# Padding the row counts of DMA loads to multiples of 16 or 15, and issuing a second table behind the first on one queue

## Chip, cores, metric

One core of one Trainium2 chip. The metric is the device time of one execution in microseconds (us), lower is better.

## The reference, cut to what matters

```python
X = np.fft.fft(np.fft.fft(x, axis=1), axis=2).real   # x: (8, 3008, 256) float32
h = X.reshape(24064, 256) @ w_in                     # (256, 2048)
g = np.maximum(h, 0.0) ** 2
out = g @ w_out                                      # (2048, 256)
```

The kernel folds the symmetric parts of the sequence together, multiplies by cosine and sine tables on TensorE, and then runs the two-layer block. Eight batches follow one another; while one is in the block, the next one's transform is slipped in between.

## The kernel before: what the change and the argument touch

```python
def class_tiles(S):                 # S = 3008: rows of x in 7 tiles by residue class
    half = S // 8 + 1
    tiles = []
    for c, order in enumerate((range(0, half, 4), range(2, half, 4), range(1, half, 2), range(half, S // 4 + 1))):
        for r in range(0, len(order), P):
            tiles.append((c, order[r], order.step, len(order[r:r + P])))
    return tiles                    # row counts: 95, 94, 128, 60, 128, 128, 120
...
    def load_x(b, t):
        _, r0, step, rows = TILES[t]

        pool, tag = (gp, "g") if b == 0 and t < NT - NX else (xp, "x")
        xt[b, t] = pool.tile([P, 4, D], F32, name="xt", tag=tag)
        nc.sync.dma_start(out=xt[b, t][0:rows], in_=x[b, r0:r0 + step * (rows - 1) + 1:step])
...
    for t in range(NT):
        load_x(0, t)

    def load_table(tab, src, engine):

        for t, (c, r0, step, rows) in enumerate(TILES):
            for i, (s0, count) in enumerate(row_tiles(S)):
                mine = [...]        # rows of this source tile that belong to tile t
                if mine:
                    o = (s0 + mine[0] - r0) // step
                    nk = NC[0][c]
                    engine.dma_start(out=tab[o:o + len(mine), :, PLACE[t]:PLACE[t] + nk],
                                     in_=src[mine[0]:mine[-1] + 1:step, :, i, 0:nk])

    load_table(cosT, cos_s, nc.sync)
    make_identity(nc, ident)
    load_table(sinT, sin_s, nc.gpsimd)
...
    for t in range(4):
        for_p(t)                    # VectorE folds four x tiles
    groups_at(0, 4)                 # TensorE: cosine products of the first classes
    for_p(4)
    groups_at(1, 2)                 # VectorE joins them (ScalarE has copied one part)
    for_p(5)
    ...
```

A row of an x tile is one run of 4096 bytes. A table is loaded in twelve pieces, of 32, 32, 31, 32, 32, 30, 64, 64, 60, 128, 128 and 120 rows; the first nine serve the first product. After the tables the sync queue loads the weights.

## Time and profile before

| | before |
|---|---|
| median time, 4 runs | 2087.41 us (2086.92 to 2092.67) |
| span of the profiled run | 2090.3 us |
| granted TensorE clock, mean | 0.987 |
| first matmul | 33.14 us |
| ScalarE's first copy of a product | 36.02 us |

In these lines PE is TensorE, DVE VectorE, ACT ScalarE, POOL GpSimd, and SPq the sync engine's queue of DMA issues. A profile line of a wait reads: who waited, for whom, us in total, times, longest. The page's account of the DMA queues has packets, MB and the share of 16 engines; q1 is the hardware queue that sync feeds, q0 the software queue of GpSimd:

```profile
q1 hardware_dynamic: 64030, 65.06, 10.7%
q0 software_dynamic: 752, 1.57, 0.3%
```

q0 holds the sine table and nothing else. Two instructions serve as milestones below: ScalarE's first copy (the first product is done) and the start of VectorE's second conversion of a raw weight (its second instruction that writes fd from raw: the head's folds and joins are done, the phase that converts weights has begun). Timeline lines have start, length, engine, line, operation and tiles:

```profile
36.02 0.24 ACT L353 COPY da<-pd 128x95 f32<-128x95 f32 x1 [34.00 <-PE pd L345]
```
```profile
64.01 0.42 DVE L201 TENSOR_SCALAR fd<-raw 128x512 uint32<-128x512 uint32 x1
```

### The profile page before, as it was taken

The numbers are of one execution on the slowest core, as the hardware profiler recorded it, in microseconds if no ns is written. First come the engines' busy times: TensorE is split into PE (matmuls) and PEld (weight loads), VectorE is DVE, ScalarE is ACT, GpSimd is POOL, SyncE is SP. The second block draws the span as 40 slices with busy tenths as digits, with TensorE's granted clock in tenths as the row PEclk, the third lists the DMA queues.
The fourth block names the chain that finished last, engine by engine and source line by source line (L and its number), as shares of the span: only waits on it lengthen the run. The fifth ranks groups of instructions, "written<-read, shape, count | busy, mean of one in ns | idle before, by whom it ended". The sixth has DMA issues, their size and how long they took to land.

```text
span 2090.3 us, 27087 instructions
## 1 busy us (share of the span) xinstructions
PE 2011.9 (96%) x9464; PEld 1748.1 (84%) x9464; DVE 1333.7 (64%) x3271; ACT 949.2 (45%) x1069; POOL 1211.9 (58%) x1778
## 2 busy tenths in 40 slices
PE   3789999999999999999999999999999999999997
PEld 1578887888888888888888888888888888888887
DVE  4688855777557765677556775577656775555553
ACT  0364434454445444444444544454444454344443
POOL 1157644676457665566546765576646665456654
PEclk9789999999999999999999999999999999999999
DMA  6124100010001000110000110011001100000000
GB/s 164 61 77 56 46 10 26 25 45 31 10 31 40 29 27 11 40 40 26 30 26 25 37 38 11 25 41 32 28 11 38 42 11 19 27 11 10 21 11 20
DMA packets 64918, 68.35 MB, mean 33 GB/s; under 512 B 25802, under 2 KB 55519, under 8 KB 64782
## 3 DMA queue, kind: packets, MB, share of 16 engines
q1 hardware_dynamic: 64030, 65.06, 10.7%
q0 software_dynamic: 752, 1.57, 0.3%
q8 instruction: 74, 1.21, 0.2%
q14 instruction: 62, 0.51, 0.1%
HBM read 41.93 MB, written 24.68 MB: 32 GB/s over the span
## 4 chain that ended last, share of the span: by engine, by line
PE 94%; DVE 3%; DMA 2%; ACT 1%; issue 0%; POOL 0%; POOLq 0%; ACTq 0%; SPq 0%; DVEq 0%
PE ph L405 16%; PE ph L406 16%; PE mA L445 16%; PE mC L445 15%; PE mB L445 15%; PE mD L445 8%; PE pd L345 5%; PE po L479 2%; DMA xt<-in_x_dram 1%; PE pg L229 1%; ACT os L481 0%; DMA cosT<-in_cos_s_dram 0%; PE pe L235 0%; DVE fd L211 0%; DVE fs L213 0%
## 5 line engine op out<-in xcount | busy, mean ns | idle before, releaser
L419 ACT ACTIVATE g<-g 128x1004 f32<-128x1004 f32 (+1 forms) x384 | 399.4, 1040 | 832.3 <-DVE g L411 549.9
L408 DVE SCALAR_TENSOR_TENSOR he<-Et,gE,ph 128x251 f32<-128x251 f32 (+1 forms) x768 | 361.9, 471 | 596.7 <-PE ph L406 596.1
L425 POOL TENSOR_TENSOR s<-g 128x251 f32<-128x251 f32 (+1 forms) x384 | 251.6, 655 | 688.7 <-ACT g L420 661.9
L405 PE MATMUL ph<-Pt,G 128*128 128x251 f32 (+1 forms) x1536 | 455.4, 377 | 0.4 <-DVE g L411 0.4
L406 PE MATMUL ph<-Qt,G 127*128 127x251 f32 (+1 forms) x1536 | 453.7, 376 | 0.0
L420 ACT ACTIVATE g<-g 128x1004 f32<-128x1004 f32 (+1 forms) x384 | 399.3, 1040 | 12.1
L445 PE MATMUL mA<-g,wout 128*128 128x251 f32 (+1 forms) x1536 | 389.9, 375 | 0.0
L445 PE MATMUL mC<-s,wsum 128*128 128x251 f32 (+1 forms) x1536 | 389.4, 374 | 0.0
L410 DVE TENSOR_TENSOR g<-he,ph 128x251 f32<-128x251 f32 (+1 forms) x768 | 320.5, 417 | 58.9 <-DVE he L408 0.5
L405 PEld LDWEIGHTS ph<-Pt,G 128*128 128x128 f32 x1536 | 289.4, 190 | 42.5 <-issue 3.2
L406 PEld LDWEIGHTS ph<-Qt,G 127*128 127x128 f32 x1536 | 292.9, 191 | 36.6
L445 PEld LDWEIGHTS mC<-s,wsum 128*128 128x128 f32 x1536 | 291.6, 190 | 35.2
L445 PEld LDWEIGHTS mA<-g,wout 128*128 128x128 f32 x1536 | 285.5, 189 | 40.1 <-issue 4.0
L411 DVE TENSOR_TENSOR g<-he,ph 128x251 f32<-128x251 f32 (+1 forms) x768 | 314.1, 409 | 0.0
L426 POOL TENSOR_TENSOR s<-s,g 128x251 f32<-128x251 f32 (+1 forms) x384 | 288.0, 750 | 30.1
L427 POOL TENSOR_TENSOR s<-g 128x251 f32<-128x251 f32 (+1 forms) x384 | 291.2, 758 | 0.0
L428 POOL TENSOR_TENSOR s<-g,s 128x251 f32<-128x251 f32 (+1 forms) x384 | 262.9, 685 | 0.0
L445 PE MATMUL mB<-g,wsum 128*128 128x251 f32 (+1 forms) x768 | 225.1, 374 | 0.0
L445 PE MATMUL mD<-s,wout 128*128 128x251 f32 (+1 forms) x768 | 225.0, 374 | 0.0
L445 PE MATMUL mB<-s,wout 128*128 128x251 f32 (+1 forms) x768 | 224.6, 374 | 0.0
L445 PEld LDWEIGHTS mB<-g,wsum 128*128 128x128 f32 x768 | 145.6, 190 | 17.8
L445 PEld LDWEIGHTS mD<-s,wout 128*128 128x128 f32 x768 | 144.9, 189 | 18.1
(74 smaller groups left out, 1327.8 us busy)
## 6 DMA issues: line engine op xcount, KB each, us to landing
xt<-in_x_dram SPq DMA_DIRECT2D x24, 512.0 KB
out_dram<-os SPq DMA_DIRECT2D x96, 125.0 KB
out_dram<-os SPq DMA_DIRECT2D x80, 126.0 KB
Et<-e_dram SPq DMA_DIRECT2D x7, 752.5 KB
raw<-in_moe_w_in_dram SPq DMA_DIRECT2D x16, 256.0 KB
raw<-in_moe_w_out_dram SPq DMA_DIRECT2D x16, 256.0 KB
xt<-in_x_dram SPq DMA_DIRECT2D x8, 480.0 KB
xt<-in_x_dram SPq DMA_DIRECT2D x8, 380.0 KB
```

Source lines behind the costliest of these rows:

```text
L405: nc.tensor.matmul(hP, G1[:, fs], pt[:, ks], start=True, stop=True)
L406: nc.tensor.matmul(hQ, G2[:, fs], qt[:, ks], start=True, stop=True)
L408: nc.vector.scalar_tensor_tensor(out=t, in0=et[:, ks], scalar=gE[:, fc:fc + 1], in1=hP, op0=ALU.mult, op1=ALU.add)
L410: tt(out=g[:, h, 0, 0:n], in0=t, in1=hQ, op=ALU.add)
L411: tt(out=g[:, h, 1, 0:n][:, ::-1], in0=t, in1=hQ, op=ALU.subtract)
L419: act(v, v, AF.Relu)
L420: act(v, v, AF.Square)
L425: gt(out=s1, in0=g21, in1=g22, op=ALU.add)
L426: gt(out=s2, in0=s1, in1=g11, op=ALU.subtract)
L427: gt(out=s3, in0=g11, in1=g21, op=ALU.subtract)
L428: gt(out=s4, in0=g12, in1=s2, op=ALU.subtract)
L445: nc.tensor.matmul(acc[nm][:, i, 0:n], w, v[:, 0:n], start=j == 0 and i == 0, stop=j == NJ - 1, skip_group_check=True)
```

## The change

Intent: let each load of x and each table piece run on all the DMA engines, by loading one or two rows more that nothing reads, and keep the sine table, which is needed late, from competing with x and the cosine table.

```diff
     def load_x(b, t):
         _, r0, step, rows = TILES[t]
 
+        while rows % 15 and rows % 16 and r0 + step * rows < NROW:
+            rows += 1
+
@@ load_table
-                    o = (s0 + mine[0] - r0) // step
+                    o, m = (s0 + mine[0] - r0) // step, len(mine)
+                    while m % 15 and m % 16 and o + m < P and mine[0] + step * m < P:
+                        m += 1
                     nk = NC[0][c]
-                    engine.dma_start(out=tab[o:o + len(mine), :, PLACE[t]:PLACE[t] + nk],
-                                     in_=src[mine[0]:mine[-1] + 1:step, :, i, 0:nk])
+                    engine.dma_start(out=tab[o:o + m, :, PLACE[t]:PLACE[t] + nk],
+                                     in_=src[mine[0]:mine[0] + step * (m - 1) + 1:step, :, i, 0:nk])
@@
-    load_table(sinT, sin_s, nc.gpsimd)
+    load_table(sinT, sin_s, nc.sync)
```

The loads of 95 and 94 rows become 96 in every batch, and the table piece of 31 rows becomes 32. Nothing else changes its shape.

## The prediction

> **What bounds the kernel now.** I began with the page's chain (part 4) to see which engine sets the end, then read the waits and the table of stretches to see where TensorE does not run, then the chain in order of time for that place alone, then the waits of the DMA queue to see why.
>
> ```profile
> PE 94%; DVE 3%; DMA 2%; ACT 1%; issue 0%; POOL 0%; POOLq 0%; ACTq 0%; SPq 0%; DVEq 0%
> ```
>
> TensorE is the bound of the whole, and DMA holds 2% of the chain. The stretches of time (us, then busy us per engine, granted clock, DMA share, GB/s) say where that 2% lies:
>
> ```profile
> 0.00:10.00 10.00, 0.00 (x0) 0.00 (x0) 1.86 (x7) 1.28 (x1) 7.21 (x16) 1.00 0.68 171
> 10.00:20.00 10.00, 0.00 (x0) 0.00 (x0) 0.00 (x0) 0.00 (x0) 1.80 (x3) 1.00 1.04 214
> 25.00:33.00 8.00, 0.00 (x0) 0.00 (x0) 6.70 (x20) 0.00 (x0) 0.00 (x0) 1.00 0.21 62
> 60.00:90.00 30.00, 22.61 (x71) 16.05 (x71) 14.15 (x32) 10.38 (x23) 0.00 (x0) 0.68 0.16 53
> 1000.00:1100.00 100.00, 98.65 (x464) 84.19 (x463) 53.04 (x141) 42.50 (x48) 51.27 (x79) 1.00 0.06 21
> ```
>
> No matmul runs before 33 us. Late in the kernel TensorE is 98.65 of 100 us busy and the DMA engines are at 0.06. So only the head can be shortened by faster transfers. Its waits, in total, times and longest (first two lines: compute engines; last: the sync DMA queue):
>
> ```profile
> PE pd L345 <- DMA cosT<-in_cos_s_dram: 33.1, 1, 33.1
> DVE fs L293 <- DMA xt<-in_x_dram: 22.2, 3, 16.4
> ```
> ```profile
> SPq L160 <- DMA xt<-in_x_dram: 16.9, 4, 13.6
> ```
>
> The third line is the key: the issue of the cosine table (L160) itself waits for a load of x. The chain in order of time (start, us):
>
> ```profile
> 1.18 23.59 DMA xt<-in_x_dram
> 24.77 0.02 issue
> 24.79 8.10 DMA cosT<-in_cos_s_dram
> ...
> 33.14 2.86 PE pd L345 x8
> ```
>
> One x load, issued at 1.18 us, lands at 24.77, and only then is a piece of the cosine table issued, which lands at 32.89. The trace names both: the load is the second, of 94 rows; the piece is the third of twelve, of 31 rows. The queue reuses eight completion semaphores in turn, so transfer number n waits for number n-8: piece 3 (transfer 10) waits for load 2.
>
> **What the Trainium skill says.** "DMA: Bandwidth & Descriptors", section "Why a DMA increments its semaphore by 16 and not by 1": the number of engines is the largest k up to 16 that divides the slowest dimension of both sides, on this path the lowest-numbered k; the queue writes the other 16-k counts at once. The trace agrees. The 95-row load shows one early update at 1.25 us and five from 5.73 to 6.53 (k=5); the 94-row load one at 1.59 and two, at 24.11 and 24.77 (k=2); the 31-row piece has k=1; 60 and 120 rows give 15. The same page, "Queues, rings and completion order", has an engine consume descriptors in ring order. That also shows: of the third load's 16 counts, 14 came between 6.40 and 9.06 and two at 26.46 and 26.86, behind the 94-row load on its two engines. The last x load had 13 engine counts by 20.32 and its last two at 30.87 and 31.34. Same page, "Issuing engines are not separate DMA queues": transfers from sync and GpSimd share the 16 engines; here the sine table's packets lie in the same microseconds (2 to 26) as those of x. "TensorE: Matmul & The Clock Gate", Part 1: the clock is halved until activity releases it; the trace has 0.68 granted in 60 to 90 us and 1.00 later.
>
> **The change part by part.**
> *Rows of x.* 95 and 94 become 96: six rows (4096 bytes each) on each of 16 engines instead of 19 on five and 47 on two. Engine 1 now carries 19+47+8+4+8+8+8 = 102 of the first batch's rows, an engine from 5 up 36. After, an engine carries 6+6+8+4+8+8+8 = 48. I counted packets in the trace in slices of 2 us: from 4 to 8 us, all engines at work, 4096-byte packets took 210 to 241 ns each and 504 and 451 KB of x moved per slice. So 48 rows take 48 x 0.24 = 11.5 us; packets flow from about 2.3 us, so the last x load lands at about 14.5 instead of 31.34. The extra row costs 12 KB in all, 0.05 us.
> *Rows of the table.* Only one piece changes, 31 rows to 32 (k 1 to 16); 30 rows stay at 15, the rest at 16 or 15. Its own 8.10 us (62 descriptors of 380 bytes behind engine 0's backlog) go below those of its neighbours.
> *Sine to the sync queue.* Twelve issues of about 0.63 us, 7.5 us of queue, and 1.52 MB move from beside x to after the cosine; at some 250 KB per us this is 6 us of transfer. It frees x of 1.57 MB of competing packets; GpSimd does not need its 12 issues' time.
>
> *What first sets TensorE going.* The first group needs nine cosine pieces. Pieces 8 and 9 are issued when the last x load and piece 1 have landed. Before: x complete 31.34, piece 9 issued 32.02, landed 34.26 (2.9 us after x), the first result copied by ScalarE at 36.02 (1.76 us more). After: 14.5 + 2.9 + 1.76 = 19.2. The gain at this point is 36.02 - 19.2 = 16.8 us; I take 16.
>
> *Does it last?* From 36 to 58 us the chain is VectorE folding and joining (14.05 of 15 us busy in 45 to 60), in fixed order, and it moves as a block. Next needs, each moved 16 us earlier: odd cosine product at 41.78, so 25.8; last cosine piece landed 39.91, 8.6 us after x, so 23.1: 2.7 us to spare. Sine product at 55.83, so 39.8; the last sine issues come at about 26 and land near 31: 8 us to spare. First weights used at 58.79, so 42.8; their issue moves from 36.6 to about 29 and they landed 5.4 us after issue, so 34.5: 8 us to spare. The next weights wait for x buffers that VectorE frees, so they move along. Nothing gives the 16 back, and after 137 us TensorE runs at full clock to the end. In later batches the x loads get shorter too, but TensorE waits for no DMA there: 0.
>
> Sum: 2087.3 - 16 = **2071 us**, 0.8% faster.
>
> **Rivals.**
> (1) *Sine in the way.* If its 7.5 us of issue stood before something needed, the gain would be 16 - 7.5 = 8.5: 2079 us. For it: the queue is one, in order, and weights stand behind. Against: the 8 us to spare above.
> (2) *Bandwidth.* If 16 engines at work slow each other: 10 to 20 us had 214 GB/s at share 1.04. Then 3.02 MB take 14.1 us, x lands at 16.4, the gain is 14: 2073. For it: 4096-byte packets took 240 to 290 ns with all engines at work and only some 150 with two. I put half of this in, by taking 16 and not 16.8.
> (3) *VectorE takes the place of DMA.* Its four folds before the first join last 7.1 us (26.88 to 28.68 is one, 1.8) and need loads 1 to 4. Load 4 ends with row 24 of 48, at 2.3 + 24 x 0.24 = 8, so folds end near 10, a fifth near 13, before 19.2. It would bind only if x came still faster; then no more than some 6 us would be left to win.
> (4) *Clock.* Between 52 and 137 us the clock alternates between half and full in steps of 3.4 us, 48 us at half in all. One such step more or less costs 3.4/2 = 1.7 us where TensorE is on the path. A moved phase can give 2 or 3 us either way; the runs before already spread from 2086.92 to 2092.67.
>
> **Range and chances.** 2071 with 2 us either way for the landing of x and 3 to 4 for clock and noise, more room upward for rival 1: 2065 to 2078. Two per cent is 41.7 us, more than the 33 us for which TensorE stands idle at the start, so faster by over 2% gets 0.01. Slower by 2% would need a new wait in the TensorE-bound part, to which the change adds nothing: 0.01. Same: 0.98.
>
> **What would show it.** Right: the seven loads of x land in order, the last near 14.5 us; the wait of the queue's L160 for x falls from one of 13.6 us to several of 1 or 2; the first matmul comes near 16 to 17 us and ScalarE's first copy near 19; the software queue q0 disappears; the sequence up to 137 us is the old one, 16 us earlier; the stretch 1000:1100 is unchanged. Wrong: a first matmul still waiting after 22 us (bandwidth or issue), a wait of TensorE or VectorE for the sine table or raw weights of some us (rival 1), or a head that is 16 us shorter while the total is not (clock or a wait later on).

## The result, and the profile after

The median of four runs is **2069.3 us** (2067.63 to 2071.05), against 2087.41 before. The ratio is 0.9908, 95% interval 0.989 to 0.9926. Ratios here are the mean time of one kernel's fast runs over that of the other's in the same rounds, so not quite the ratio of the medians quoted. By a 2% rule this is "the same"; the 0.9% is clear of the noise.

The page of the changed kernel has no q0 any more; the chain holds less DMA:

```profile
q1 hardware_dynamic: 65968, 66.73, 11.4%
```
```profile
PE 94%; DVE 3%; DMA 1%; ACT 0%; issue 0%; SPq 0%; POOL 0%; POOLq 0%; ACTq 0%; DVEq 0%
```

The waits up to 110 us, of the compute engines and then of the sync queue:

```profile
PE pd L350 <- DMA cosT<-in_cos_s_dram: 16.2, 2, 15.5
...
DVE fs L298 <- DMA xt<-in_x_dram: 4.0, 1, 4.0
```
```profile
SPq L165 <- DMA xt<-in_x_dram: 7.4, 7, 1.7
SPq L165 <- DMA cosT<-in_cos_s_dram: 1.1, 1, 1.1
```

TensorE's wait for the cosine table is halved, and the queue's four waits for x, one of them of 13.6 us, have become seven with a longest of 1.7. The chain in order of time:

```profile
3.51 11.18 DMA xt<-in_x_dram
14.71 2.52 DMA cosT<-in_cos_s_dram
17.23 0.14 issue
17.36 1.91 PE pd L350 x4
19.30 0.25 ACT da L358
```

The x load on the chain is now the last one, issued at 3.51, no longer the second. The cosine piece behind it is the eighth, which waits for the last load's completion count as before.

When each load of x was complete, from the semaphore updates in the two traces (us). A load is complete at 16 counts; each engine that carries part of it adds one when its part is there, and the counts that no engine will add come at once (the prediction shows this for loads of 95 and 94 rows). So the number of late counts is the number of engines:

| load | rows | engines before | complete before | rows after | complete after |
|---|---|---|---|---|---|
| 1 | 95 | 5 | 6.53 | 96 | 4.84 |
| 2 | 94 | 2 | 24.77 | 96 | 6.13 |
| 3 | 128 | 16 | 26.86 | 128 | 8.06 |
| 4 | 60 | 15 | 27.48 | 60 | 9.30 |
| 5 | 128 | 16 | 28.75 | 128 | 10.34 |
| 6 | 128 | 16 | 30.02 | 128 | 12.35 |
| 7 | 120 | 15 | 31.34 | 120 | 14.69 |

Five loads that the change does not touch end 17 to 19 us earlier. The milestone of the weights:

```profile
47.98 0.42 DVE L206 TENSOR_SCALAR fd<-raw 128x512 uint32<-128x512 uint32 x1
```

It is 16.03 us earlier than before. But the profiled spans differ by 23.2 us (2090.3 to 2067.1). Between about 64 and 140 us of the kernel before, the two profiles part by another 6.9 us. The stretches show where (columns as in the prediction's table of stretches: length, then busy us of PE, of PE's weight loads, of DVE, ACT and POOL; the clock is the third number from the end):

```profile
60.00:90.00 30.00, 19.24 (x68) 15.82 (x69) 23.42 (x44) 18.24 (x31) 9.10 (x15) 0.74 0.32 95
90.00:120.00 30.00, 25.47 (x117) 21.52 (x116) 27.63 (x49) 19.97 (x33) 15.67 (x24) 0.92 0.32 99
...
120.00:140.00 20.00, 20.00 (x99) 17.90 (x98) 18.25 (x38) 11.25 (x17) 15.16 (x25) 1.00 0.31 67
```

and the kernel before in the later two:

```profile
90.00:120.00 30.00, 21.37 (x68) 17.11 (x67) 24.15 (x44) 17.45 (x28) 12.81 (x21) 0.72 0.27 88
120.00:140.00 20.00, 17.94 (x75) 15.43 (x76) 17.45 (x31) 11.97 (x21) 10.50 (x16) 0.83 0.35 106
```

This profile of the kernel before had 47.8 us at half clock ahead of its steady part, that of the changed kernel 30.7. (The traces hold no record of the clock before 41.76 and 26.65 us; the 1.00 of earlier stretches is no measurement.) Four of the 6.9 us can be followed on the two chains: from the second weight conversion to the third they have the same links, and the same 14 matmuls took, before and after,

```profile
72.02 6.67 PE pd L345 x14
```
```profile
55.08 3.49 PE pd L350 x14
```

The clock records have half clock from 65.65 to 79.31 us in the first trace and full clock from 53.96 to 60.79 in the second. With two shorter groups of matmuls this makes 4.1 us, and the third conversion starts 20.1 us earlier instead of 16.0. The experiments show that which execution meets how much of this is chance and no part of the change. From 204 us on nothing more is won or lost: between fixed VectorE instructions the two traces differ by 22.92 us at 204 us, 22.87 at 537 and 22.86 at 1636, and the stretch from 1000 to 1100 us has the same busy TensorE:

```profile
1000.00:1100.00 100.00, 98.65 (x466) 85.09 (x466) 55.24 (x142) 42.86 (x49) 54.68 (x83) 1.00 0.07 21
```

### The profile page after: what moved, and what is told of

Same layout as the page of the kernel before. It is cut to its first block, busy times and chain, and to the rows that moved or that the text cites. A ratio compares the mean times of both kernels' runs of the same rounds, so it can differ in the third digit from the quotient of the medians.

```text
span 2067.1 us, 27083 instructions
## 1 busy us (share of the span) xinstructions
PE 2004.5 (97%) x9464; PEld 1742.9 (84%) x9464; DVE 1334.7 (65%) x3271; ACT 949.4 (46%) x1069; POOL 1202.6 (58%) x1766
## 4 chain that ended last, share of the span: by engine, by line
PE 94%; DVE 3%; DMA 1%; ACT 0%; issue 0%; SPq 0%; POOL 0%; POOLq 0%; ACTq 0%; DVEq 0%
PE ph L410 16%; PE mA L450 16%; PE ph L411 16%; PE mC L450 16%; PE mB L450 15%; PE mD L450 8%; PE pd L350 5%; PE po L484 2%; PE pg L234 1%; DMA xt<-in_x_dram 1%; ACT os L486 0%; DVE he L413 0%; PE pe L240 0%; DVE g L416 0%; DVE g L415 0%
## 5 line engine op out<-in xcount | busy, mean ns | idle before, releaser
L450 PEld LDWEIGHTS mD<-s,wout 128*128 128x128 f32 x768 | 144.9, 189 | 18.1
```

Of the source, the lines that this page charges most:

```text
L450: nc.tensor.matmul(acc[nm][:, i, 0:n], w, v[:, 0:n], start=j == 0 and i == 0, stop=j == NJ - 1, skip_group_check=True)
```

## The experiments

The theory: loads of 95 and 94 rows run on five and two engines; engines work in order, so every later transfer with a share on engines 0 and 1 waits behind them. Rivals: the sine packets beside x are the whole cause; the single-engine table piece is; the queue's wait for a completion count is; or a load lands by its bytes, whatever the engines. All heads are read from one profile a run; the spread of ScalarE's first copy is some 0.9 us (19.30 and 20.20 for the changed kernel, profiled twice). Times are medians. All outputs are right. The kernel before had 2086.68 us beside e1 to e4, 2087.43 beside e5 to e8, and 2087.02 beside e9 and e10 (the last is the seven runs of the second and one more).

### e1: x rows alone

```diff
 # from the changed kernel
-                    while m % 15 and m % 16 and o + m < P and mine[0] + step * m < P:
-                        m += 1
-    load_table(sinT, sin_s, nc.sync)
+    load_table(sinT, sin_s, nc.gpsimd)
```

> Only the rows of x are padded; table rows and the sine table (GpSimd queue) as before. Theory (the backlog of engines 0 and 1, made by the loads of 95 and 94 rows, holds the head): the last x load lands near 17.5 us instead of 31.3 (48 rows per engine, beside some 0.7 MB of sine), the 31-row piece of the cosine table on one engine costs some 2.5 us more, ScalarE's first copy comes at about 23.5 instead of 36.0: 12.5 us less, about 2075 us. Rival (the sine table's packets beside x are the main cause): x lands after 25 us, the first copy comes after 30, gain under 6 us.

Measured: 2078.53 us, ratio 0.9959 (0.9945 to 0.9974). The last x load was complete at 18.36; the first copy, in the timeline:

```profile
27.25 0.24 ACT L356 COPY da<-pd 128x95 f32<-128x95 f32 x1 [25.23 <-PE pd L348]
```

That is 8.8 us earlier than before, more than the sine rival allows and less than the 12.5 that I expected. x itself landed close to the 17.5 expected; the nine cosine pieces took 7.0 us more (25.35), against 3.0 in the whole change. They now move beside the large sine pieces, the last of which landed at 23.38, and the 31-row piece on one engine landed at 24.15; e5 tells the two apart in part.

### e2: table rows alone

```diff
 # from the kernel before
+                    while m % 15 and m % 16 and o + m < P and mine[0] + step * m < P:
+                        m += 1
```

> Only the one table piece of 31 rows is made 32, on both tables. Theory: nothing, as its 8.1 us on the chain were spent behind the backlog of engine 0 and its neighbours end no earlier: the first copy at 36.0 us as before (within 1), time within 2 us of the kernel before. Rival (the single-engine piece itself is slow): the first copy comes 3 us or more earlier.

Measured: 2084.66 us, ratio 0.9994 (0.9975 to 1.0013). The first copy came at 34.63, 1.4 us earlier, just outside what I expected and not far from the spread. But x, which this edit does not touch, was complete at 29.99 instead of 31.34, and the ninth cosine piece came 2.9 us after x, as before. So the whole 1.4 us came with x, and none of it behind x, where the cosine piece stands. Load 2 was in (24.14 instead of 24.77) before that piece was issued; the padded sine piece beside x, or chance, is what is left, and no run tells these apart.

### e3: sine table alone

```diff
 # from the kernel before
-    load_table(sinT, sin_s, nc.gpsimd)
+    load_table(sinT, sin_s, nc.sync)
```

> Only the sine table moves behind the cosine on the sync queue; x loads stay at 95 and 94 rows, the table piece at 31. Theory: engine 1 still carries 102 rows of x, at 0.2 us each while all engines work and 0.15 when two are left, so the last x load lands near 20 to 21 us, the first copy at about 25.5: some 10.5 us less, about 2077 us. If sine packets beside x cost nothing: the first copy stays at 36. Together with the x-only run this tells how far the two parts overlap: 12.5 and 10.5 do not add up to the 16.7 of both.

Measured: 2078.96 us, ratio 0.9968 (0.9949 to 0.9988). x complete at 23.02, first copy at 27.76: 8.3 us earlier. The chain of this run still has the 94-row load in it, shorter:

```profile
1.17 16.11 DMA xt<-in_x_dram
17.30 7.29 DMA cosT<-in_cos_s_dram
```

```profile
27.76 0.24 ACT L353 COPY da<-pd 128x95 f32<-128x95 f32 x1 [25.74 <-PE pd L345]
```

So the sine packets beside x did cost, and the rows too. The packets of the kernel before show how: from 22 to 26 us, 27 packets of x of 4096 bytes started, beside 18 large ones of the sine table; from 26 to 30 us, after the last sine packet (25.92), 49 did. Each took about as long in both stretches (170 and 163 ns on average); they took turns. I had expected the two parts to overlap; with 8.8 and 8.3 they add up to 17.1, and both together gave 16.7.

### e4: the change without its table rows

```diff
 # from the changed kernel
-                    while m % 15 and m % 16 and o + m < P and mine[0] + step * m < P:
-                        m += 1
```

> The change without its table rows: x padded, sine behind cosine, but the piece of 31 rows on one engine. Theory: 62 descriptors of 380 bytes on engine 0, about 40 ns each, put 2.5 us of backlog on that engine ahead of six cosine pieces: the first copy at about 21.3 us instead of 19.3, total about 2 us above the whole change (2071). Rival (31 rows or 32 are the same once x is even): the first copy within 0.5 us of 19.3.

Measured: 2072.34 us (2068.31 to 2076.73), ratio 0.9929 (0.9906 to 0.9952). My expectation was wrong: the first copy came at 19.28, not 21.3. The piece of 31 rows landed at 15.04, between its neighbours (14.94 and 15.22). The median above 2069 is the clock, told below: two of the four runs had it at 0.986.

### e5: the change with the sine table back on GpSimd

```diff
 # from the changed kernel
-    load_table(sinT, sin_s, nc.sync)
+    load_table(sinT, sin_s, nc.gpsimd)
```

> The change without its third part: x and table rows padded, the sine table still on the GpSimd queue beside x. In the x-only run (first copy 27.25 us) the 31-row piece of the cosine table landed at 24.15, 3.6 us after the piece before it, and the pieces behind it ended on that one engine at 24.3 to 25.35, while three engines lagged anyhow (24.17 for the next slowest). Theory: taking that piece off the one engine lets the ninth cosine piece land at about 24.2 and the first copy come at about 26.1, 1.1 us earlier than with x alone; the other 7 us to the whole change (19.3) come from the sine packets that still run until some 23 us. Rival (the one-engine piece is what held the x-only run): the first copy near 22.

Measured: 2078.84 us (2074.61 to 2082.94), ratio 0.9958 (0.9937 to 0.998). Two of its four runs were long ones (clock 0.986 and 0.987, told under e9), so the median says little beside that of e1. The first copy came at 26.35, where 26.1 was expected:

```profile
26.35 0.24 ACT L358 COPY da<-pd 128x95 f32<-128x95 f32 x1 [24.33 <-PE pd L350]
```

The rival is out: with all rows even, the sine table beside x and the cosine still costs 6.2 to 7.1 us (26.35 against 20.20 and 19.30). The number was reached by another way than I had thought, though: x was complete only at 20.49 (18.36 in e1, with the same x rows), and the ninth cosine piece, at 24.40, came 3.9 us after x instead of 7.0. So the even piece may well have saved some 3 us behind x, of which the later x took 2; one profile each does not settle it.

### e6: cosine table ahead of x

```diff
 # from the kernel before
-    for t in range(NT):
-        load_x(0, t)
     ...
     load_table(cosT, cos_s, nc.sync)
+    for t in range(NT):
+        load_x(0, t)
```

> From the kernel before, only the order: the cosine table is issued ahead of the x loads, which keep 95 and 94 rows; sine on GpSimd. It takes away the wait of the cosine issue for the 94-row load, and leaves the load on two engines. Theory (engines 0 and 1 work through 102 rows of x): the four x loads for the first group still end near 33 us, as the cosine is now ahead of them; first copy at 35 to 37 as before (36.0), time within 4 us of the kernel before. Rival (the queue's wait for a completion count holds the head): the first copy comes before 26 us, time 10 us or more lower.

Measured: 2094.74 us, ratio 1.0035 (1.0018 to 1.0052). The nine pieces were there at 8.28 us, and yet:

```profile
39.86 0.24 ACT L352 COPY da<-pd 128x95 f32<-128x95 f32 x1 [37.83 <-PE pd L344]
```
```profile
DVE fs L292 <- DMA xt<-in_x_dram: 30.8, 2, 23.8
PE pd L344 <- DMA xt<-in_x_dram: 26.4, 1, 26.4
```

Without the wait of the cosine issue TensorE waits for x itself, longer than before, as x is now issued from 7.80 us on instead of 0.75: load 2 landed at 33.51, and the third and fourth behind it at 34.76 and 35.39. The queue's wait was how the backlog reached the table, not its cause. The first copy was 2.9 us later than I had allowed.

### e7: one load of 97 rows

```diff
 # from the changed kernel, in load_x
+        if b == 0 and t == 1:
+            rows = 97
```

> The whole change with one load made worse: the second x load takes 97 rows, a prime, so by the rule of the largest divisor up to 16 all 97 run on one engine (a dose of the suspected cause; results stay right). Theory: that engine has 139 rows where the others have 42; at 0.23 us a row while all work and 0.16 when it is alone (as in the sine-only run), the load lands near 22 us, the last x load near 28, the first copy at about 32.5 instead of 19.3. Rival (landing goes by the bytes of the load, one row more): all within 0.5 us of the whole change.

Measured (one run): 2084.11 us. Load 2 complete at 22.75, the last load at 28.53, the first copy at 33.15. The chain:

```profile
8.59 19.94 DMA xt<-in_x_dram
28.54 2.54 DMA cosT<-in_cos_s_dram
```
```profile
33.15 0.24 ACT L360 COPY da<-pd 128x95 f32<-128x95 f32 x1 [31.14 <-PE pd L352]
```

One row more than the 96 of the change, 1% more bytes, delays that load by 16.6 us and the first copy by 13.9. The semaphore had one data update for this load. So this load landed with its fullest engine and not by its size.

### e8: the change without its x rows

```diff
 # from the changed kernel
-        while rows % 15 and rows % 16 and r0 + step * rows < NROW:
-            rows += 1
```

> The change without its first part: table rows padded, sine behind cosine, x loads still 95 and 94 rows. The sine-only run gave x complete at 23.02 and the first copy at 27.76, with the ninth cosine piece 2.9 us after x. Theory: that piece waits for the last x load, not for the 31-row piece (landed 24.59), so the table rows add nothing: first copy 27.7, within 0.4. Rival (the table rows matter where x is late): 1 us or more earlier.

Measured (one run): 2077.09 us. The first copy at 27.66 (27.7 expected), the last x load at 23.07. Beside e3 the table rows add 0.1 us.

### e9: the change again

No edit.

> The whole change again, unaltered, for its spread and as the base of the next run. First copy at 19.3 us within 0.5, second weight conversion (the second of VectorE's reads of a raw weight) at 48.0 within 0.7. Theory of the rest of the measured gain: from that conversion to the 1000th VectorE instruction a run takes either about 465.7 us (31 to 34 us of half clock in its head) or about 472.6 (48 to 51 us), whatever the kernel; the profile of the kernel before fell in the long kind and that of the change in the short one. So both kinds appear here: times near 2069 at a mean granted clock of 0.990 or more, and near 2075 at 0.986.

Measured: 2070.13 us in four runs (2069.2 to 2070.81), ratio 0.9917 (0.99 to 0.9933). Three of my expectations failed: the first copy came at 20.20, 0.4 us outside what I gave, and the second conversion at 48.89, 0.2 us outside; and only the short kind of run appeared here, so the changed kernel itself has not shown the long kind in its eight runs. The later first copy goes with x: complete at 15.59 instead of 14.69, as some engines lagged (load 6: eleven counts by 11.59, five from 12.71 to 14.44). The table has every profile:

| profile | second conversion | from there to a fixed VectorE instruction near 514 to 540 us | half clock before steady part | mean clock of run |
|---|---|---|---|---|
| before | 64.01 | 472.5 | 47.8 | 0.987 |
| after | 47.98 | 465.7 | 30.7 | 0.991 |
| e1 | 56.68 | 466.1 | 34.1 | 0.990 |
| e2 | 63.31 | 465.5 | 30.7 | 0.991 |
| e3 | 56.45 | 465.9 | 30.7 | 0.991 |
| e4 | 47.74 | 472.7 | 51.2 | 0.986 |
| e5 | 54.67 | 472.7 | 51.2 | 0.986 |
| e6 | 71.89 | 466.7 | 41.0 | 0.988 |
| e7 | 61.91 | 466.6 | 30.7 | 0.990 |
| e8 | 56.34 | 465.6 | 30.7 | 0.991 |
| e9 | 48.89 | 465.5 | 30.7 | 0.991 |
| e10 | 46.53 | 466.6 | 34.1 | 0.989 |

Two kinds, 466 and 472.6 us, nothing between, and no relation to the edit: e4 differs from the changed kernel by one row in two table pieces and fell in the long kind. The kernel before has both kinds among its timed runs: of 19, fourteen took 2084.86 to 2087.51 us and five 2091.19 to 2092.67, with nothing between. The mean clock of a run tells them apart less well: runs at 0.988 are in both groups.

### e10: first group's transfers ahead of the others

```diff
 # from the changed kernel
-    for t in range(NT):
+    for t in range(4):
         load_x(0, t)
-    def load_table(tab, src, engine):
+    def load_table(tab, src, engine, part=range(NT)):
         for t, (c, r0, step, rows) in enumerate(TILES):
+            if t not in part:
+                continue
-    load_table(cosT, cos_s, nc.sync)
+    load_table(cosT, cos_s, nc.sync, range(4))
+    for t in range(4, NT):
+        load_x(0, t)
+    load_table(cosT, cos_s, nc.sync, range(4, NT))
@@
-    for_p(4)
     groups_at(1, 2)
+    for_p(4)
```

> A version that might beat both: the whole change, with the four x loads and nine cosine pieces of the first group ahead of the last three x loads and the large cosine pieces, and VectorE's first joins ahead of its fifth fold. The ninth piece is issued near 10.2 us and lands near 12 instead of 17.7, ScalarE's first copy comes near 13.6 instead of 19.3. VectorE then still owes the fifth fold (1.8 us), so its line moves 3.9 us, if the last cosine piece lands by about 21: second weight conversion at 44.1 instead of 48.0, time 2065.5 against 2069.3. Rival (bandwidth: the same bytes must land before the odd product): the last cosine piece still lands at 23, and the gain is 1 to 2 us.

Measured: 2068.87 us in six runs (2067.2 to 2074.24), ratio 0.9914 (0.9899 to 0.9929). The ninth piece landed at 12.18 and the first copy came as expected:

```profile
13.73 0.24 ACT L363 COPY da<-pd 128x95 f32<-128x95 f32 x1 [11.72 <-PE pd L355]
```
```profile
46.53 0.42 DVE L211 TENSOR_SCALAR fd<-raw 128x512 uint32<-128x512 uint32 x1
```

But the second conversion is only 1.5 to 2.4 us earlier than in the two profiles of the change: the rival was right. The last cosine piece landed at 22.58 (23.03 and 23.48 there): the same bytes had to be in, and TensorE waited for the large cosine pieces instead. The chain of this run has 9.17 us of cosine table from 12.54 on, which is the eleventh piece, landed at 21.70 (20.98 and 21.92 there). Of the 5.6 to 6.5 us won at the first copy most was given back at these transfers. In timed runs the gain isn't resolved: the intervals of the ratios of e9 and e10 overlap almost wholly.

### What the parts are worth

ScalarE's first copy in the eight combinations (us):

| sine table | no padding | table rows | x rows | both |
|---|---|---|---|---|
| GpSimd, beside x | 36.02 | 34.63 (e2) | 27.25 (e1) | 26.35 (e5) |
| sync, behind cosine | 27.76 (e3) | 27.66 (e8) | 19.28 (e4) | 19.30, 20.20 (e9) |

The x rows are worth 7.5 to 8.8 us in each row of the table, the sine move 6.2 to 8.3 in each column, the table rows from about 0 to 1.4. Two profiles of one kernel differ by 0.9, and the landing of x in e1 and e5 by 2.1, so the worth of the table rows is not shown to be other than 0.

## Why the prediction was right

Its steps, in its own order:

- **Only the head can gain.** Held: from 204 us to 1636 us the traces keep their distance within 0.06 us, though the x loads of seven later batches run on more engines too.
- **48 rows on each engine land by 14.5 us.** Held: 14.69 (15.59 in the second profile). That it is as close as 0.2 us is partly luck. The packet times given for 4 to 8 us (210 to 241 ns) are not in the trace, where the 2 us slices average 222 and 286; the changed kernel had 194 to 238 from 2 to 12 us, but its first x packet came at 1.76 us instead of 2.3, and the last engine ended well after the first (14.69 against 12.90). e7 tests the same count of rows with 139 on one engine: 28 expected, 28.53 measured.
- **Ninth piece 2.9 us after x, first copy at 19.2.** Held: 17.70 is 3.0 after 14.69; the copy came at 19.30, and 16.7 us were gained there (15.8 in the second profile). The first matmul came at 15.49, a little before the 16 to 17 given: TensorE starts on the first table pieces and then waits for the eighth (landed at 17.23).
- **It moves as a block.** Held: 16.03 us at the second conversion (15.1 in the second profile). Of the reserves, the last cosine piece was expected at 23.1 and landed at 23.03, the sine table near 31 and 31.66, the first weights at 34.5 and 33.98. Rival 1 (sine in the way) did not come about.
- **Rival 2 (bandwidth)**, half of which I had taken in by putting 16 for 16.8, was not needed in the first profile and about right in the second. Its 3.02 MB should be 3.10 (756 rows), which puts x at 16.8 instead of 16.4. **Rival 3 (VectorE)** stayed away: four folds ended at 12.0 instead of 10, the fifth at 13.9 instead of 13, both well before 19.2.
- **The table piece.** The text gave it no gain of its own apart from its neighbours; the runs give 0 to 1.4 us. Right, but my later expectation that it would cost 2 us within the change (e4) was not.
- **The clock.** That the clock could give or take some us was right; the size was not. I worked with single steps of 1.7 us and allowed 2 or 3; the runs have two kinds 6.9 us apart (472.6 against 465.7 in the table). The profile of before was of the long kind, which is why the profiled spans differ by 23.2 us and not by 16.
- **The sum.** 16 us were predicted from the head, 18.1 measured between medians. Runs of the same mean clock of 0.991 give 16.5: before 2085.74, 2086.03, 2086.61, 2086.4 and 2084.86 (mean 2085.9), changed 2068.87, 2067.63, 2069.64, 2069.2, 2070.61 and 2070.81 (mean 2069.5). All fourteen short runs of the kernel before (mean 2086.6) and all eight of the changed kernel (2069.7) give 16.9. The rest of the 18.1 is spread within the short kind, and chance. 2069.3 lies within 2065 to 2078.

One reading of the trace was off without consequence: the sine packets lie between 5.93 and 25.92 us, not from 2 on (their issue begins at 1.54).

What the prediction did not do was to share the gain between the parts, and there my first guesses (12.5 for x, 10.5 for sine, overlapping) were off: 8.8 and 8.3, adding up. An explanation would be that both lengthen the same line of work on the fullest engine; that is argued, not shown, as the trace does not name the engine of a packet. In e1 the last three of a load's counts lagged by up to 1 to 2 us (load 6: thirteen by 13.52, the last three from 14.55 to 15.15) with no row count to explain it, and so it did in the second profile of the change, with no sine table beside x; which engines these are, and why, stays open.

## What to carry to other kernels

Look at the row counts of loads before their sizes: a count whose largest divisor up to 16 is small put the whole load on few engines here (95, 94, 97 and 31 rows on 5, 2, 1 and 1), and what followed on those engines waited behind it, also loads that were spread well; one or two unused rows repaired it. A transfer that is needed late belongs behind the ones needed early, on the same queue: on another queue it took turns with them. And before a difference of some us between two profiles is explained, compare the granted clock in the same stretch: here 6.9 of the 23.2 us between the profiled spans were no part of the change, and 4.1 of them are matmuls at half clock on the chain.

## What the Trainium skill lacked or had wrong

- "DMA: Bandwidth & Descriptors", "Why a DMA increments its semaphore by 16 and not by 1", gives the number of engines, and the runs agree (5 for 95 rows, 2 for 94, 1 for 97 and 31, by the updates of the semaphores). It lacks the cost for what is queued behind: a 94-row load on two engines delays the end of a 128-row load issued behind it from about 9 us (fourteen of its counts were in by 9.06) to 26.86.
- The same page, "Issuing engines are not separate DMA queues", says that issuing from several engines saves only issue time. It does not say that it can cost: the sine table from GpSimd instead of behind the cosine on sync, the same bytes on the same engines, made the first product 6 to 8 us later (seen from e3 and e5).
- The same page, "Specifications", has some 27 GiB/s for one engine. Packets of 4096 bytes took 162 to 163 ns on average where two engines were at work (26 to 30 us of the kernel before), which is 25 GB/s, a little less. Where all 16 were at work, a slice of 2 us averaged 194 to 238 ns (2 to 12 us of the changed kernel, 256 to 341 GB/s in all). The row is for one engine; that table has other rows for all of them together, so this second number is no gap.
- "TensorE: Matmul & The Clock Gate", Part 1, describes the half clock and calls it variable from run to run; the steps of 3.4 us agree. It lacks that here, where the head leaves TensorE idle in part, whole executions fall into two kinds: 31 to 41 us or 48 to 51 us at half clock over twelve profiles, with 465.5 to 466.7 and 472.5 to 472.7 us over one fixed stretch; and that one kernel has both (e4: 2068.31 and 2069.06, then 2075.62 and 2076.73).
